# Two transformer layers, one new token each: what stays in SBUF between the layers

## Chip, cores and metric

One core of a Trainium2 chip runs the whole program. The metric is device time in microseconds of one execution; the kernel before has a median of 875.19 us in three runs.

## What is computed

Eight sequences (B=8) of one new token each, D=1024, go through the same two blocks twice, with the same weights and the same caches both times. All is float32.

```
for layer in 0, 1:
    n = layernorm(x)
    q = n @ wq                                   # 1024 x 4096, 32 heads of 128
    s = q . k_cache * 128**-0.5                   # 4 kv heads, 4096 positions; 8 query heads share one
    x = x + concat(softmax(s) . v_cache) @ wo     # 4096 x 1024
    n = layernorm(x)
    x = x + gelu(n @ w1 + b1) @ w2 + b2           # 1024 x 3584, 3584 x 1024
```

Each weight and each cache is read twice, once per layer. Per layer wq and wo are 16 MB each, w1 and w2 14 MB each, K and V 64 MB each (MB = 2^20 bytes), so 188 MB. SBUF holds about 24 MB at a time. Whatever is still there when layer 1 needs it isn't loaded again; the softmax has no mask, so the order in which batches are worked is free, and layer 1 goes through them backwards.

## The kernel before

**The arena.** One SBUF tile, `arena` (L110), is cut into units of 128 partitions x 1024 float32, 0.5 MB each. There are 52: 48 for loads (`N_TILE = 24` pairs) and 4 own ones, for score rows and probabilities. `Arena.take` (L62) hands out k adjacent units, those freed longest ago first; a `Slot` gives them back. A "piece" of a cache is two units: one kv head, half of the positions.

**The stream.** `stream` is a list of all loads in the order in which they are to be issued, built by `weights` (L495) and `caches` (L506). `pump` (L210) takes entries from its head while there is room, and issues a DMA for each on SP's queue (L221). It is called at each `release`, that is, where the program frees a tile. The program is written out beforehand, so the order on SP's queue is fixed; at run time each DMA waits until the engines that read its slot before have done so. One entry without room holds up all behind it.

**Compute.** Weight tiles stream through TensorE as the moving operand, with four groups of 32 output rows beside each other. `expand` (L237) multiplies the normed x with wq or w1, in two halves; `project` (L304) the heads with wo, or the hidden values with w2, tile by tile, and adds to x (L323). `scores` (L343) takes one piece of K in four matmuls (L352); after four pieces VectorE scales a half and takes the maximum (L357). `probs` and `turn` (L364, L376) make the softmax and turn the rows (L366 to L392), `values` (L393) takes a piece of V in four matmuls (L402), and VectorE puts the heads together (L405, L407, L414, L415). `layernorm` (L181) turns x and runs a mean; the variance is taken while the first matmuls of `expand` run. `plan` (L433) lists the steps of attention: for most batches all of K, softmax, all of V; for the last two or three of a layer K of one batch is mixed with V of the one before, with a lag of ten pieces.

**Loads.** In the attention of layer 0 a load is a whole batch's K or V, 8 MB, except for batches 6 and 7, which `CUTS` divides into 2 MB and 1 MB tiles. wo, w1, w2 of layer 0 and wq of layer 1 come in 1 MB tiles (a few of 0.5). In layer 1 the caches grow from 1 MB back to 8 MB, and wo, w1, w2 come in 16-, 14- and 8-unit tiles, with w2 ending in small ones.

**What is kept.** Between the layers 23 pieces stay: K and V of batch 7 and seven of the eight pieces of K of batch 6; one of them is parked in PSUM (`park_tile`, L478) and copied back later (`unpark`, L490). The last 1536 columns of wq stay in `spare` (L553). While they lie there, 4 units of the 48 and, once attention is over (`opened`, L486), the 4 own ones are left for the weights: a ring of 4 MB. Layer 1 starts with scores on kept pieces between the parts of its second half of wq (`early`).

x, b1 and b2 are loaded by three DMAs (x from ACT's queue, L129; the biases from SP's, L537).

Of the kernel before, what the change touches and what calls it, by code (L numbers as in the profile page):

```python
# [14 lines left out]
P = 128  # L15
# [6 lines left out]
CH = 512  # L22
# [11 lines left out]
LAG_V = 10  # L34

SCW = W // 2
N_TILE = 24
N_OWN = 2
EXTRA = 7
AT_ONCE = range(6), range(5)  # L40
CUTS = {
    (0, "k", 6): (2, 2, 2, 1, 1), (0, "v", 6): (2, 2, 2, 2), (0, "k", 7): (1, 1, 2, 1, 1, 2), (0, "v", 7): (2, 2, 2, 1, 1),
    (1, "k", 6): (2, 2, 2, 1, 1), (1, "v", 6): (1, 1, 2, 2, 2), (1, "k", 5): (1, 1, 1, 1, 2, 2), (1, "v", 5): (4, 4), (1, "k", 4): (4, 4),
}
# [6 lines left out]
class Arena:  # L51


    def __init__(self, ap):
        self.ap = ap
        self.low = 2 * N_TILE
        self.n = self.low + 2 * N_OWN
        self.freed = dict.fromkeys(range(self.n), 0)
        self.clock = 0
        self.limit = self.cap = self.low  # L60

    def take(self, k=1, own=False, pack=False):  # L62
        low = self.low if own else 0
        high = self.n if own else self.limit
        if k == 0:
            return Slot(self, 0, 0)
        able = [i for i in range(low, high - k + 1, k) if all(i + e in self.freed for e in range(k))]
        if not able:
            return None
        whole = lambda i: all(i // 4 * 4 + e in self.freed for e in range(4))  # L70
        i = min(able, key=lambda i: (pack and whole(i), max(self.freed[i + e] for e in range(k)), i))
        for e in range(k):
            self.freed.pop(i + e)
        return Slot(self, i, k)


class Slot:
    def __init__(self, arena, i, k):
        self.arena, self.i, self.k = arena, i, k
        self.cols = k * SCW  # L80
        self.ap = arena.ap[:, i * SCW:(i + k) * SCW]

# [6 lines left out]
class Kept:  # L89


    def __init__(self, ap):
        self.ap, self.cols = ap, ap.shape[1]
# [6 lines left out]
def decode_layers(ctx: ExitStack, tc: tile.TileContext, x, kc, vc, wq, wo, w1, b1, w2, b2, out):  # L100
# [9 lines left out]
    arena = Arena(const.tile([P, 2 * (N_TILE + N_OWN) * SCW], F32, name="arena"))  # L110
# [15 lines left out]
    x_row = const.tile([P, Q4], F32, name="x_row")  # L126
    bT = const.tile([P, NFT + NT], F32, name="bT")
    b1T, b2T = bT[:, 0:NFT], bT[:, NFT:]
    nc.scalar.dma_start(out=x_row, in_=x)  # L129
# [80 lines left out]
    def pump():  # L210
        while stream:
            key, k, src, limit, pack = stream[0]
            arena.limit = min(limit, arena.cap)
            slot = arena.take(k, pack=pack)
            if slot is None:
                return
            stream.pop(0)
            if callable(src):
                src(slot.ap)
            else:  # L220
                nc.sync.dma_start(out=slot.ap[:, 0:src.shape[1]], in_=src)  # L221
                slot.cols = src.shape[1]
            held[key] = slot

    def release(slot):
        slot.free()
        pump()
# [76 lines left out]
    def project(name, n_k, lhs, out_row, resid, rsum, hooks={}):  # L304
        y = ps_o.tile([P, CH], F32, tag="o", name="y")
        kt = 0
        for i, slot in enumerate(tiles(name)):
            for c in range(0, slot.cols, D):
                for j in range(4):
                    nc.tensor.matmul(y[32 * j:32 * j + 32, 0:Q4], lhs[:, kt * B:kt * B + 32],  # L310
                                     slot.ap[:, c + j * Q4:c + (j + 1) * Q4],
                                     start=(kt == 0), stop=(kt == n_k - 1))
                kt += 1
                if kt in hooks:
                    hooks[kt]()
                if name[0] == "p" and kt == 2 * NT:
                    add_b2(y)
                if kt == NR:
                    flush()
            release(slot)  # L320
            flush()
        assert kt == n_k
# [20 lines left out]
    def scores(at, kt, spare=False):  # L343
        b, j, half = at
        if j == 0:
            st["ps", half] = ps_o.tile([P, CH], F32, tag="o", name="s_ps") if spare else small_ps("s")
# [7 lines left out]
        if j == HKV - 1:  # L354
            if half == 0:
                st["row", b] = arena.take(own=True)
# [19 lines left out]
    def turn(b, half):  # L376
        row = st["row", b].ap
        if half == 0:
            st["S", b] = arena.take(own=True)
# [48 lines left out]
    def early(key):  # L428
        ap, done = ap_of(key)
        scores(key[1:], ap, spare=key[3] == 1)  # L430
        done()

    def plan(layer, order):  # L433

        steps = []
        for i, b in enumerate(order):
            n = i * NR
            whole = b in AT_ONCE[layer]
            steps.append((n + NR - whole, 1, ("probs", b)))
            steps.append((n + NR + 1 - 2 * whole, 2, ("turn", b)))  # L440
            for r in range(NR):
                steps.append((n + r, 0, ("k", *k_at(b, r))))
                steps.append((n + NR - 1, 3, ("v", *v_at(b, r))) if whole else (n + r + LAG_V, 3, ("v", *v_at(b, r))))
        steps.sort(key=lambda e: e[:2])
        return [key for _, _, key in steps]

    def attention(order, keep, done=(), hooks={}):
        ready = []
        steps = [key for key in plan(st["layer"], order) if key not in done]
        for n, key in enumerate(steps):  # L450
            if n == 0 and done:
                flush()
# [25 lines left out]
    def park_tile():  # L478
        spot = ps_k.tile([P, W], F32, name="spot")
        ap, done = ap_of(park)  # L480
        nc.scalar.activation(spot[:, 0:W // 2], ap[:, 0:W // 2], AF.Copy)
        nc.vector.tensor_copy(spot[:, W // 2:], ap[:, W // 2:])
        st["spot"] = spot
        done()

    def opened():  # L486
        arena.cap = arena.n
        pump()

    def unpark(ap):  # L490
        spot = st.pop("spot")
        nc.scalar.activation(ap[:, 0:W // 2], spot[:, 0:W // 2], AF.Copy)
        nc.vector.tensor_copy(ap[:, W // 2:], spot[:, W // 2:])

    def weights(name, dram, sizes, limit, short=(0, 0)):  # L495

        for u in range(dram.shape[0]):
            at = 0
            for i, k in enumerate(sizes[u]):
                n = min(k * SCW, dram.shape[2] - short[u] - at)  # L500
                key = ((name, u) if dram.shape[0] > 1 else name, i)
                stream.append((key, k, dram[u, :, at:at + n], limit[u], False))
                at += n
            assert at == dram.shape[2] - short[u]

    def caches(layer, order, skip):  # L506

        for key in plan(layer, order):
            if key[0] not in "kv" or key in skip:
                continue  # L510
            a, b = key[:2]
            lane = [(a, *(k_at if a == "k" else v_at)(b, r)) for r in range(NR)]
            at = lane.index(key)
            cuts = CUTS.get((layer, a, b), (NR,))
            starts = [sum(cuts[:i]) for i in range(len(cuts))]
            if at not in starts:
                continue
            m = cuts[starts.index(at)]
            name = (layer, key)
            for i, e in enumerate(lane[at:at + m]):  # L520
# [101 lines left out]
```

## Time and profile before

| what | us |
|---|---|
| median of 3 runs | 875.19 |
| lowest, highest | 874.1, 876.13 |
| span of the profiled execution (its own time is this span; no other time of it was taken) | 874.0 |
| TensorE busy in the span | 537.3 |
| VectorE busy | 182.3 |
| ScalarE busy | 48.8 |

The page gives, first, the busy time of each engine, then the span in 40 slices of 21.85 us with what the 16 DMA engines moved in each (GB/s). The chain of waits goes back from the last instruction to whatever released each step; in order of time its rows are: start in us, length in us, what it was (engine, tile, line, how many). In the timeline the bracket at a row's end says how long the engine had been idle and what ended that. In the table of windows the last three columns are the clock granted to TensorE (1.00 is full), the mean busy share of the DMA engines and GB/s. In a group of matmuls each matmul of the program appears twice, as float32 is worked in two passes.

### The profile page before, as it was taken

What the parts mean: (1) busy time and instruction counts of PE and PEld (TensorE: products, weight loads), DVE (VectorE), ACT (ScalarE), POOL (GpSimd) and SP (SyncE); (2) the same over time, 40 slices, a digit from 0 to 9 for tenths busy, and PEclk for the clock granted to TensorE, in tenths of its full rate; (3) what the DMA queues carried; (4) which work ended last, traced back from release to release, by engine and by line L of the source; (5) the groups of instructions that cost most, each with busy time, mean ns of one, the idle gap of its engine ahead of it and who ended that gap; (6) DMA issues with size and microseconds to landing.
All of it is one profiled execution on the core that took longest, in us unless ns stands there. A gap on an engine that the chain in (4) does not pass through costs nothing.

```text
span 874.0 us, 9060 instructions
## 1 busy us (share of the span) xinstructions
PE 537.3 (61%) x4000; PEld 179.4 (21%) x4000; DVE 182.3 (21%) x588; ACT 48.8 (6%) x76; POOL 1.7 (0%) x11
## 2 busy tenths in 40 slices
PE   0556665655657756666666879764665655665566
PEld 0212121211212212222221122211121211222223
DVE  0001232313122322200110134312232313120011
ACT  0110000000000100000000100000000000000000
POOL 0000000000000000000000000000000000000000
PEclk9977788777787977869978699886878777777878
DMA  9999999999999999999999999999999999999996
GB/s 389 434 432 430 432 439 439 438 436 436 432 430 406 426 426 426 403 407 419 421 421 412 418 423 432 431 445 430 439 432 433 430 432 430 433 432 436 426 424 287
DMA packets 19911, 370.22 MB, mean 424 GB/s; under 512 B 2464, under 2 KB 2720, under 8 KB 4128
## 3 DMA queue, kind: packets, MB, share of 16 engines
q1 hardware_dynamic: 19728, 369.52, 99.1%
q8 instruction: 31, 0.51, 0.2%
q10 hardware_dynamic: 144, 0.13, 0.0%
q14 instruction: 8, 0.07, 0.0%
HBM read 369.51 MB, written 0.13 MB: 423 GB/s over the span
## 4 chain that ended last, share of the span: by engine, by line
DMA 75%; PE 19%; DVE 4%; issue 1%; ACT 1%; SPq 0%; ACTq 0%; DVEq 0%
DMA arena<-in_A_v_cache_dram 25%; DMA arena<-in_A_k_cache_dram 24%; DMA arena<-in_B_w_dram 16%; PE sps L352 5%; PE o_ps L402 5%; DMA arena<-in_A_wo_dram 5%; PE acc L252 4%; DMA arena<-in_A_wq_dram 3%; DMA x_row<-in_A_x_dram 3%; PE y L310 2%; DVE scr L407 2%; PE sps L414 1%; PE sps L383 1%; DVE scr L405 1%; DVE arena L357 0%
## 5 line engine op out<-in xcount | busy, mean ns | idle before, releaser
L352 PE MATMUL sps<-arena,qz 128*32 128x512 f32 x992 | 146.1, 716 | 92.8 <-DMA arena<-in_A_k_cache_dram 82.7
L402 PE MATMUL o_ps<-arena 128*32 128x512 f32 x1024 | 155.5, 721 | 30.5 <-DMA arena<-in_A_v_cache_dram 30.4
L310 PE MATMUL y<-arena,oxT 128*32 128x256 f32 x960 | 80.4, 481 | 48.4 <-DMA arena<-in_A_wo_dram 29.6
L252 PE MATMUL acc<-arena,oxT 128*32 128x512 f32 (+3 forms) x522 | 77.8, 661 | 45.7 <-DMA arena<-in_B_w_dram 28.0
L407 DVE SCALAR_TENSOR_TENSOR scr<-o_ps,bits,scr 128x128 f32<-128x128 f32 x192 | 67.3, 350 | 6.8
L352 PEld LDWEIGHTS sps<-arena,qz 128*32 128x32 f32 x992 | 30.8, 125 | 181.6 <-issue 79.3
L310 PEld LDWEIGHTS y<-arena,oxT 128*32 128x32 f32 x960 | 34.2, 132 | 92.3 <-DMA arena<-in_A_wo_dram 32.3
L357 DVE TENSOR_SCALAR_CACHE_REDUCE arena<-sps 128x512 f32<-128x512 f32 x31 | 21.4, 691 | 151.4 <-PE sps L352 151.4
L402 PEld LDWEIGHTS o_ps<-arena 128*32 128x32 f32 x1024 | 31.2, 126 | 100.7 <-issue 65.4
L383 PE MATMUL sps<-ident,arena 128*128 128x128 f32 x128 | 29.9, 376 | 32.5 <-DVE oxT L415 16.8
L373 ACT ACTIVATE arena<-arena,bits 128x1024 f32<-128x1024 f32 x16 | 18.4, 1147 | 476.4 <-DVE scr L370 476.4
L414 PE MATMUL sps<-bits,scr 128*128 128x8 f32 x128 | 26.2, 277 | 28.5 <-DVE scr L407 24.8
L405 DVE TENSOR_SCALAR scr<-o_ps,bits 128x128 f32<-128x128 f32 x64 | 22.4, 351 | 91.6 <-PE o_ps L402 91.6
L252 PEld LDWEIGHTS acc<-arena,oxT 128*32 128x32 f32 x522 | 19.5, 122 | 95.2 <-issue 34.1
L414 PEld LDWEIGHTS sps<-bits,scr 128*128 128x128 f32 x128 | 20.4, 200 | 86.0 <-DVE scr L407 65.0
L383 PEld LDWEIGHTS sps<-ident,arena 128*128 128x128 f32 x128 | 19.3, 188 | 42.3 <-ACT arena L373 23.9
L415 DVE TENSOR_TENSOR oxT<-sps,scr 128x8 f32<-128x8 f32 x64 | 11.0, 171 | 79.8 <-PE sps L414 79.8
L389 DVE COPY arena<-sps 128x512 f32<-128x512 f32 x16 | 11.1, 691 | 44.1 <-PE sps L383 44.1
L184 PE MATMUL sps<-ident,x_row 128*128 128x128 f32 x16 | 4.0, 338 | 24.9 <-DMA x_row<-in_A_x_dram 23.2
L323 DVE SCALAR_TENSOR_TENSOR x_row<-y,x_row 128x256 f32<-128x256 f32 x4 | 1.7, 425 | 81.2 <-PE y L310 81.2
L391 PE MATMUL sps<-scr,bits 128*128 128x32 f32 x32 | 9.5, 388 | 12.5 <-DVE arena L389 12.5
L366 PE MATMUL sps<-scr,bits 128*128 128x128 f32 x32 | 7.8, 326 | 15.1 <-DVE scr L362 15.1
(71 smaller groups left out, 135.0 us busy)
## 6 DMA issues: line engine op xcount, KB each, us to landing
arena<-in_B_w_dram SPq DMA_DIRECT2D x27, 1024.0 KB, 8.4
arena<-in_A_v_cache_dram SPq DMA_DIRECT2D x10, 2048.0 KB, 29.2
arena<-in_A_wo_dram SPq DMA_DIRECT2D x15, 1024.0 KB, 8.6
arena<-in_A_k_cache_dram SPq DMA_DIRECT2D x7, 2048.0 KB, 29.5
arena<-in_A_wq_dram SPq DMA_DIRECT2D x14, 1024.0 KB, 8.0
arena<-in_B_w_dram SPq DMA_DIRECT2D x2, 7168.0 KB, 44.7
arena<-in_A_k_cache_dram SPq DMA_DIRECT2D x11, 1024.0 KB, 27.0
arena<-in_A_k_cache_dram SPq DMA_DIRECT2D x2, 4096.0 KB, 27.1
```

The source lines that it names most:

```text
L252: nc.tensor.matmul(acc[32 * j:32 * j + 32, d0 - starts[j]:d1 - starts[j]], xnT[:, kt * B:kt * B + 32], slot.ap[:, c + d0 - a:c + d1 - a], ...
L310: nc.tensor.matmul(y[32 * j:32 * j + 32, 0:Q4], lhs[:, kt * B:kt * B + 32], slot.ap[:, c + j * Q4:c + (j + 1) * Q4], start=(kt == 0), stop ...
L352: nc.tensor.matmul(ps[32 * g:32 * g + 32, :], qz[:, c:c + 32], kt[:, g * CH:(g + 1) * CH], start=(j == 0), stop=(j == HKV - 1))
L357: nc.vector.tensor_scalar(st["row", b].ap[:, half * CH:(half + 1) * CH], ps, SCALE, None, op0=ALU.mult, op1=ALU.max, accum_out=st["mx", b] ...
L373: nc.scalar.activation(row, row, AF.Exp, bias=bias, scale=1.0, accum_out=ls)
L383: nc.tensor.transpose(pp[:, t * P:(t + 1) * P], row[:, c:c + P], ident)
L389: nc.vector.tensor_copy(dst, src)
L402: nc.tensor.matmul(o[32 * g:32 * g + 32, :], s[:, g], v[:, g * CH:(g + 1) * CH], start=(half == 0), stop=(half == NH - 1))
L405: nc.vector.tensor_scalar(r, o[:, 0:P], sel_t[:, 0:1], None, op0=ALU.mult)
L407: nc.vector.scalar_tensor_tensor(r, o[:, t * P:(t + 1) * P], sel_t[:, t:t + 1], r, op0=ALU.mult, op1=ALU.add)
L414: nc.tensor.matmul(po[:, 0:REP], r_s[j % 2], sel_h, start=True, stop=True)
L415: nc.vector.tensor_tensor(oT_v[:, j * REP:(j + 1) * REP, b], po[:, 0:REP], rl_s[b % 2][:, j * REP:(j + 1) * REP], ALU.mult)
```

## The change

- The arena has 52 units with fixed places: `OWN = 48` to 51 for rows and probabilities, `RING = 32` to 47 (to 51 once attention of layer 0 is over). Each entry of the stream carries the list of units at which it may start.
- Kept between the layers: the first half of wq (units 0 to 15, loaded once at the start and read tile by tile in layer 1), K of batch 7 (units 16 to 31), and the first half of w2 (units 32 to 45, loaded last in layer 0). `Slot.keys` and `parts` turn a slot that is released into kept tiles instead of freeing it. One piece of the second half of wq is parked in PSUM and `spare` holds its last 1536 columns as before; `park` and `unpark` are now at wq's end.
- All cache loads are 4 MB (8 units, half of a batch's K or V), in four slots: 16, 24, 32, 40 in layer 0 and 0, 8, 16, 24 in layer 1. Only V of batch 7 in layer 0 ends in two 2 MB tiles.
- wo, w1 and w2 of layer 0 come in 2 MB tiles (with shorter last ones) through units 32 to 51; in layer 1 in 4 MB tiles through units 0 to 31.
- In layer 0 w2 is read second half first (`ks`), after both halves of the hidden values are there (`flush`); in layer 1 in order, so that the kept half comes first.
- Attention works whole batches only: K, softmax, V. `early`, `CUTS`, `AT_ONCE` and the lag are gone.
- x, b1 and b2 are put into one array beforehand and come in one DMA.

```diff
+N_UNIT = 52
+OWN = 48
+RING = 32
+R_AT = (46, 48, 50)
+KV_AT = (16, 24, 32, 40), (0, 8, 16, 24)
+HALF_AT = (32, 36, 40, 44), ()
...
+    def take(self, k, starts):
+        able = [i for i in starts if all(i + e in self.freed for e in range(k))]
...
+    def parts(self):
+        k = self.k // len(self.keys)
+        return [(key, Slot(self.arena, self.i + e * k, k)) for e, key in enumerate(self.keys)]
...
     def release(slot):
+        if slot.keys:
+            held.update(slot.parts())
+            return
         slot.free()
         pump()
...
+    def plan(order):
+
+        for b in order:
+            yield from (("k", *k_at(b, r)) for r in range(NR))
+            yield ("probs", b)
+            yield ("turn", b)
+            yield from (("v", *v_at(b, r)) for r in range(NR))
...
+    kept = {("k", *k_at(B - 1, r)) for r in range(NR)}
     orders = [list(range(B)), list(range(B))[::-1]]
+    ring = lambda k, i: range(RING, N_UNIT - k + 1, k)
+    deep = lambda k, i: range(0, RING - k + 1, 8 if k > 4 else k)
+    fixed = lambda *at: lambda k, i: (at[i],)
+    last_q = [2] * 5 + [2.5]
+    early = NFT // 2
+
+    weights(("q0", 0), wq[0], [16], fixed(0), kept=lambda i: [(("q1", 0), e) for e in range(8)])
+    weights(("q0", 1), wq[1], [16], fixed(RING))
+    stream.extend(caches(0, orders[0], (), {("v", B - 1): (4, 2, 2)}))
+    weights("o0", wo[0], [4] * 8, ring)
+    for u in range(2):
+        weights(("i0", u), w1[u], [4, 4, 4, 2], ring)
+    weights("p0", w2[0], [4, 4, 4, 2], ring, early * D)
+    weights("p0", w2[0], [4, 4, 2, 2, 1, 1], fixed(32, 36, 40, 42, 44, 45), 0, 4, lambda i: [("p1", i)])
+    weights(("q1", 1), wq[1], last_q, fixed(*R_AT, 0, 2, 4))
+    stream.extend(caches(1, orders[1], kept, {}))
+    weights("o1", wo[0], [8] * 4, deep)
+    for u in range(2):
+        weights(("i1", u), w1[u], [8, 6], deep)
+    weights("p1", w2[0], [4, 4, 2, 2, 1, 1], deep, early * D, 6)
...
+        ks = list(range(NFT))
+        if layer == 0:
+            flush()
+            ks = ks[early:] + ks[:early]
+        project(f"p{layer}", ks, hT, x_row, x_row, rsum)
```

More of the change, by code (lines that the diff above doesn't have):

```diff
@@ L506, in caches, with unpark @@
[L506 to L520, printed above, removed]
-                pieces[layer, e] = (name, i)
-            src = (kc if a == "k" else vc)[b]
-            yield (name, 2 * m, src[:, at * W:(at + m) * W], 2 * N_TILE, m == 1)
+    def unpark(key):
+        spot = st.pop("spot")
+        slot = arena.take(2, R_AT)
+        nc.scalar.activation(slot.ap[:, 0:W // 2], spot[:, 0:W // 2], AF.Copy)
+        nc.vector.tensor_copy(slot.ap[:, W // 2:], spot[:, W // 2:])
+        held[key] = slot
```

204 lines of the change are left out of this document (77 added, 127 removed).

## The prediction

> **What bounds the kernel now.** I read the first two parts of the page, then windows, then the chain of waits in order of time.
>
> ```profile
> span 874.0 us, 9060 instructions
> PE 537.3 (61%) x4000; PEld 179.4 (21%) x4000; DVE 182.3 (21%) x588; ACT 48.8 (6%) x76; POOL 1.7 (0%) x11
> ...
> GB/s 389 434 432 430 432 439 439 438 436 436 432 430 406 426 426 426 403 407 419 421 421 412 418 423 432 431 445 430 439 432 433 430 432 430 433 432 436 426 424 287
> DMA packets 19911, 370.22 MB, mean 424 GB/s; under 512 B 2464, under 2 KB 2720, under 8 KB 4128
> ```
>
> The 16 DMA engines move 370 MB at a nearly level rate, and no compute engine is busy for over 61%. In the windows below the DMA share is 1.00 and 1.01. So the kernel is one long transfer: the span changes only by what a byte costs, and by time in which the DMA queue is empty. The middle of the GB/s row (slices 12 to 23) is slower than its sides. That is the stage with short tiles. Two windows show it, and the last one the end:
>
> ```profile
> 40.00:240.00 200.00, 117.83 (x748) 37.49 (x752) 44.31 (x145) 11.96 (x17) 0.00 (x0) 0.76 1.00 432
> 390.00:460.00 70.00, 45.24 (x410) 16.36 (x414) 7.27 (x23) 3.93 (x7) 0.28 (x1) 0.87 1.01 420
> 860.00:870.00 10.00, 7.16 (x92) 3.63 (x92) 0.20 (x1) 0.00 (x0) 0.00 (x0) 0.83 0.71 292
> ```
>
> The last three columns are granted clock, DMA share and GB/s. At 390 to 460 us the DMA share is 1.01 although the ring holds only 4 MB: the small ring does not starve the engines there, the short tiles only carry less per unit of time. Prices per tile come from moments at which TensorE starts on a tile that has just landed, in the chain and, for 4 MB tiles, in the timeline of TensorE:
>
> ```profile
> 199.94 3.69 PE o_ps L402 x16
> ...
> 206.67 0.36 DVE scr L405
> ...
> 258.00 1.98 PE sps L352 x8
> ...
> 479.94 1.98 PE acc L252 x8
> ...
> 489.88 1.93 PE acc L252 x8
> ```
> ```profile
> 577.78 1.94 PE L352 MATMUL sps<-arena,qz 128*32 128x512 f32 x8 [6.03 <-DMA arena<-in_A_k_cache_dram]
> 587.49 1.06 PE L402 MATMUL o_ps<-arena 128*32 128x512 f32 x8 [2.42 <-DMA arena<-in_A_v_cache_dram]
> ```
>
> From 199.94 to 258.00 three 8 MB tiles landed: 19.35 us each. From 479.94 to 489.88 four 1 MB tiles: 2.485 each. A line through both is 2.409 us per MB (MiB) plus 0.076 us per tile; it gives 9.71 for 4 MB, and the two timeline rows are 9.71 apart. So a 2 MB tile is 4.89 and a 0.5 MB tile 1.28 (both worked out). The profile counts each matmul twice: "x32" is half a batch's K, 16 matmuls.
>
> **The change part by part.**
>
> *Bytes.* Layer 0 loads the same. Layer 1 loads, in columns of 512 bytes: before 31232 of wq, 215040 of caches, 90112 of wo, w1 and w2, together 336384; after 12800 of wq (half is kept, another part is in PSUM and the spare buffer), 245760 of caches (only one batch's K is kept), 75776 of the rest (half of w2 is kept), together 334336. That is 2048 columns or 1 MB less: -2.4 us. Much more weight is kept, and almost as much less cache.
>
> *Tiles.* The issues from SP's queue into the arena fall from 134 to 111, and the two for the biases go into the one for x: 25 fewer times 0.076 is -1.9. The cache tiles of 4 MB instead of 8 are in that count. Together -4.3.
>
> *The layers themselves.* In attention four 4 MB slots take the place of three 8 MB ones. A slot is refilled when TensorE has read it; three tiles of 9.71 us lie in between and the work on one takes under 15 us (5.64 and 8.46, below), so the queue stays full. The same holds for the 2 MB tiles of wo and w1, five slots of 4.89.
>
> *The handover from layer 0's last V to wo.* Here the queue can run dry. Half of wq sits in slots 0 to 15, the last batch's K in 16 to 31 and is kept, so the only room for wo is what the last V leaves in 32 to 47. Let t be the landing of the last half of K7. Behind it in the queue are V7 in 4, 2 and 2 MB: 9.71+4.89+4.89 = 19.5 us, and nothing else can be issued until the first V7 tile is read. That takes:
>
> ```profile
> 141.89 5.64 PE sps L352 x32
> 147.56 0.71 DVE arena L357 x2
> 148.31 3.69 PE sps L352 x32
> ...
> 638.53 0.71 DVE arena L357 x2
> ...
> 646.99 3.62 PE o_ps L402 x16
> ```
> ```profile
> out_dram<-x_row SPq DMA_DIRECT2D x1, 128.0 KB, 1.7
> ```
>
> Half of K after an idle time takes 5.64 us; the second half, without one, 3.69 (the granted clock averages 0.76 in the window 40 to 240). The softmax chain from L357 to the first value matmul is 8.46 (638.53 to 646.99). Four V pieces take 6.73 (199.94 to 206.67, where VectorE takes up the second head). Then SP issues, and the smallest transfer lands 1.7 us after its issue, of which I count 1.3 as time to the first bytes. So the first wo bytes move at t+5.64+8.46+6.73+1.3 = t+22.1, and the queue is empty from t+19.5: a stall of **2.6 us**. Ends: 0.7 with the half at 3.69, and nothing if the chain is 0.7 shorter too; with 1.4 us of delay above these rows, 4.0. In the kernel before finer tiles of two batches lie there. I take 2.6, since TensorE waits some 5 us for that half.
>
> The Trainium skill, TensorE: Matmul & The Clock Gate, section "HAM oscillation — how this bites in real kernels", says that a loop whose tile is computed faster than the next one arrives runs every tile at the low clock. It speaks against splitting K into halves that arrive apart; the rows above (5.64 against 3.69) agree, and by it the stall is 2.6, without it about 0.7. The skill's DMA: Bandwidth & Descriptors, section "Latency and other measured facts", puts the first byte at about 0.6 us for this path; by that page the stall would be 1.9, but the row of the output transfer says 1.7 to landing, and I keep it.
>
> *Stagger of the engines.* When the queue runs dry, engines that were ahead idle too and begin together again. In the window 860 to 870 the share is 0.71 before the last landing at 870.1: 2.9 us of mean stagger. What it costs has then been paid, and the engine that falls behind in the rest of the span pays again. Ends 0 and 2.9 times that rest's share (0.6) = 1.7; I take 0.5, nearer to nothing, since the span before already holds all delays of its slowest engine.
>
> *Between the layers.* Three places have cover, and cost nothing by these rows:
>
> ```profile
> 25.67 9.10 PE acc L252 x63
> ...
> 467.45 0.68 PE y L310 x8
> ...
> 470.12 1.05 PE acc L252 x4
> ```
>
> (a) Five loads of w2 and three of wq wait in SP's queue behind one slot, read out by the fourth w2 tile. If w1 ends at X, the four tiles land at X+4.9, 9.8, 14.7 and 17.2; the third and fourth are read by X+20.2 even at twice the 57 ns a record that the end shows (32 records 3.6, 16 records 1.8), bytes move by X+21.5, and the queue, with the fifth tile issued long before, lasts to X+22.1. (b) After w2's last landing three 1 MB tiles of wq run for 7.5 us. The first kept wq tile is read after 2.67 (467.45 to 470.12, the norm between) plus 1.1, and bytes move at 5.1. (c) V7's first load waits for the whole kept half of wq: 2.67+9.10+1.3 = 13.1; the queue lasts 7.5+5.0+3.1 = 15.6. Margins 0.6, 2.4 and 2.5 us. Behind (c) SP holds all further cache loads.
>
> *The end.* Only half of w2, 17.3 us of transfers, comes after w1, not 34. TensorE has to do its work in that time.
>
> ```profile
> 835.66 8.58 PE L252 MATMUL acc<-arena,oxT 128*32 128x512 f32 x64 [8.34 <-DMA arena<-in_B_w_dram]
> ...
> 853.47 0.75 PE L277 MATMUL sps<-ident,scr 128*128 128x128 f32 x4
> ...
> 855.38 3.66 PE L310 MATMUL y<-arena,oxT 128*32 128x256 f32 x64 [1.17 <-DMA arena<-in_B_w_dram]
> ...
> 860.50 0.39 PE L333 MATMUL y<-scr,bits 128*32 128x256 f32 x2
> ```
> ```profile
> 870.11 0.69 PE y L310 x8
> ```
>
> From w1's last landing v: the last 28 of 64 records 3.75, w2 by 224 records at 57 ns (3.66 over 64) 12.8, the turn 0.75, the bias 1.85 (from 859.04, where 855.38 ends, to 860.89): v+19.2. The transfers alone would allow v+17.3+0.7 (the 0.69 of the last tile) = v+18.0. So TensorE is late by **1.2**; ends 0 (with a quick start, as fast as the second half of those 64) and 4 (w2 as slow as the start of a tile after a wait).
>
> Sum: -4.3+2.6+0.5+1.2 = 0.0, so 874.0 for this execution's span of 874.0. What lies around the span is not changed. The execution stands 1.2 us under the median of 875.19; from the median the forecast is **875.2 us**.
>
> **The rivals.** (1) *The handovers are hidden.* TensorE is at speed when the last K half lands, wo starts 0.7 late, and the end is bound by transfers: -4.3+0.7 = -3.6, 871.6 us. For it: a 61% busy TensorE that has little left to do; against it the 5.64 row.
> (2) *Low clock at the handovers*, slower. The kept half of wq is read in eight pieces; rows 479.94 and 489.88 show 1.98 and 1.93 us a piece, where 25.67 has 9.10 for eight. At the slow rate V7's first bytes move at 2.67+15.6+1.3 = 19.6 instead of 13.1, 4.0 after the queue is empty. It decides once the eight take over 11.6 us (9.10 and the margin of 2.5). With 4.0 at the first handover and the rest as in the sum: -4.3+4.0+0.5+1.2+4.0 = +5.4, 880.6 us. Against it: unlike there, the pieces lie ready.
> (3) *The change doesn't do what it says*: the longer tiles are no cheaper, since the slow middle was that stage's and not the tiles'. Then the 1.9 us of the tiles is missing from the sum: +1.9, 877.1 us. The 9.71 row speaks against it.
>
> **How the numbers follow.** Forecast 0.50 (873.4 to 876.9), rival 1 0.22, rival 2 0.22, rival 3 0.06. A measurement of this kernel tells about 0.2%, 1.75 us, from no change. So faster 0.22, same 0.50, slower 0.28. The range leaves out the upper part of rival 2 and what lies under rival 1: 871.3 to 879.0. The forecast's own range is 873 to 877.
>
> **What would show it.** Right: the GB/s row level near 430 in the middle with one dip, where layer 0's attention ends; there TensorE waits for wo and SP's first wo issue follows the second V head by under 0.1 us; about 1 MB less moved; at the end TensorE runs without a wait into the last tile of w2. Wrong: no dip (rival 1), a second dip before layer 1's first V load (rival 2), about 420 GB/s in the attention windows (rival 3).

## The result, and the profile after

The kernel after takes 871.89 us (median of 5 runs, 871.26 to 872.87) beside 875.01 for the kernel before (5 runs, 874.10 to 876.13): a ratio of 0.9964, 95% interval 0.9951 to 0.9976. It is 3.1 us faster, where I had forecast no change. The spans of the two profiled executions differ by 3.4 us (874.0 and 870.6). The profiled execution of after took 872.42, 1.8 us more than its span; that distance is 1.7 to 1.9 in every later run too, so the execution of before, of which only the span is known, very likely took some 875.8. The prediction set its span of 874.0 beside the median of 875.19 and took the difference for an execution that was fast; most of it is this distance. As its sum was 0.0, the forecast doesn't change by that.

First the page of after: span, busy times, GB/s in 40 slices, DMA packets.

```profile
span 870.6 us, 9005 instructions
...
PE 554.2 (64%) x3988; PEld 191.5 (22%) x3988; DVE 182.6 (21%) x588; ACT 48.7 (6%) x76; POOL 1.7 (0%) x11
...
GB/s 391 434 434 433 432 434 428 425 434 431 427 431 431 433 434 425 388 429 430 424 409 411 436 431 431 434 433 432 429 431 428 432 431 428 431 433 430 429 425 291
DMA packets 16312, 369.17 MB, mean 424 GB/s; under 512 B 1809, under 2 KB 2065, under 8 KB 2577
```

As foretold, 1.05 MB (in millions; 1 MiB) less is moved, and the middle of the GB/s row is level but for dips (I had foretold one). The 388 in slice 16 (348 to 370 us) is the end of layer 0's attention; 409 and 411 (435 to 479) are the place between the layers. In between, where 1 MB tiles became 2 MB ones, the engines are as busy as before and carry more. Windows with granted clock, DMA share and GB/s at the end of each row, first of before, then of after:

```profile
370.00:450.00 80.00, 49.81 (x468) 17.30 (x472) 6.57 (x22) 3.93 (x7) 0.28 (x1) 0.86 1.01 416
```
```profile
370.00:450.00 80.00, 50.95 (x472) 20.39 (x468) 6.57 (x22) 3.93 (x7) 0.28 (x1) 0.82 1.01 428
```

More windows of after:

```profile
40.00:240.00 200.00, 130.96 (x774) 40.73 (x778) 47.19 (x151) 12.90 (x18) 0.00 (x0) 0.76 1.00 429
...
350.00:352.00 2.00, 2.00 (x13) 0.54 (x16) 0.36 (x1) 0.00 (x0) 0.00 (x0) 0.50 1.00 418
352.00:354.00 2.00, 2.00 (x12) 0.40 (x8) 0.35 (x1) 0.00 (x0) 0.00 (x0) 0.50 0.56 238
354.00:356.00 2.00, 1.73 (x16) 0.47 (x12) 1.23 (x5) 0.00 (x0) 0.00 (x0) 0.88 0.76 197
356.00:358.00 2.00, 1.46 (x16) 0.25 (x8) 1.23 (x4) 0.00 (x0) 0.00 (x0) 1.00 1.11 475
```

The dip is there, so the first handover isn't hidden outright. But it is small: shares of 0.56 and 0.76 over 2 us each and 1.11 behind them leave (0.44 + 0.24 - 0.11) x 2 = 1.1 us in which a DMA engine on average had nothing to do. What made it so small stands in the timeline of after (TensorE, VectorE and SP's queue; start, length, engine, line, what; in brackets the idle time before and what ended it):

```profile
336.68 5.34 PE L350 MATMUL sps<-arena,qz 128*32 128x512 f32 x32 [4.35 <-DMA arena<-in_k_dram]
...
342.07 0.69 DVE L355 TENSOR_SCALAR_CACHE_REDUCE arena<-sps 128x512 f32<-128x512 f32 x1 [8.97 <-PE sps L350]
...
349.94 5.01 PE L400 MATMUL o_ps<-arena 128*32 128x512 f32 x24
...
353.64 22.15 SPq L214 DMA_DIRECT2D arena<-in_wo_dram  x8
353.65 0.35 DVE L403 TENSOR_SCALAR scr<-o_ps,bits 128x128 f32<-128x128 f32 x1 [3.25 <-PE o_ps L400]
...
367.31 2.89 PE L308 MATMUL y<-arena,oxT 128*32 128x256 f32 x32 [2.63 <-DMA arena<-in_wo_dram]
...
396.73 1.93 PE L308 MATMUL y<-arena,oxT 128*32 128x256 f32 x32 [1.39 <-DMA arena<-in_wo_dram]
```

The last half of K7 lands at t = 336.68 and takes 5.34 us, as I had it. The chain from L355 to the first value matmul is 7.9 (342.07 to 349.94), not 8.46. The large miss is the next step. SP issues the first wo tile at 353.64, when VectorE takes up the *first* head of V7 (353.65), 3.7 us after the values begin. I had waited for the second head, 6.73 us. The program frees V7's 4 MB tile only when all four pieces are read. But the first wo tile is 2 MB and overwrites two of these pieces. In the built program the DMA waits only for the readers of what it overwrites. So the issue is at t+17.0, not t+20.8.

The rows also give what was lost there. Between 336.68 and the last wo landing, 396.73, are 60.05 us; V7 and eight wo tiles need 9.71 + 10 x 4.89 = 58.61. **The handover lost 1.4 us**, where I had 2.6 + 0.5. Below, "lost" is always this difference. The last part of the timeline is the end; the row below it is the DMA that SP issued at 834.25, w2's last tile, with the time from issue to landing:

```profile
849.48 2.78 PE L249 MATMUL acc<-arena,oxT 128*32 128x384 f32 x28 [0.26 <-DMA arena<-in_w_dram]
...
861.92 5.55 PE L308 MATMUL y<-arena,oxT 128*32 128x256 f32 x94
```
```profile
arena<-in_w_dram SPq DMA_DIRECT2D x1, 512.0 KB, 32.4
```

From w1's last landing (849.48) to the end of TensorE's work (861.92 + 5.55 = 867.47) are 18.0 us, not 19.2. The last 28 records of w1 took 2.78 instead of 3.75, and w2 made up the rest. My figure for transfers alone was 18.0 too, but that doesn't make the transfers the bound. TensorE goes through w2 without waiting for a load, as foretold, and the last tile lands at 866.65, just as TensorE comes to it: reading it takes about the last 0.8 us. In this execution both limits fall together.

So between the two profiles: -4.3 for bytes and tiles, +1.4 for the handover, nothing at the end; that is -2.9, beside the -3.4 of the spans and the -3.1 of the medians. Of the 2.9 between this and my 0.0, the handover is 1.7 and the end 1.2.

### The profile page after: what moved, and what is told of

It reads as the page before. It is cut to its first block, busy times and chain, and to the rows that moved or that the text cites. A ratio compares the mean times of both kernels' runs of the same rounds, so it can differ in the third digit from the quotient of the medians.

```text
span 870.6 us, 9005 instructions
## 1 busy us (share of the span) xinstructions
PE 554.2 (64%) x3988; PEld 191.5 (22%) x3988; DVE 182.6 (21%) x588; ACT 48.7 (6%) x76; POOL 1.7 (0%) x11
## 4 chain that ended last, share of the span: by engine, by line
DMA 75%; PE 20%; DVE 2%; issue 1%; ACT 1%; another core or an unknown queue 1%; SPq 0%; ACTq 0%; DVEq 0%
DMA arena<-in_k_dram 53%; PE sps L350 11%; DMA arena<-in_w_dram 10%; DMA arena<-in_wo_dram 7%; DMA arena<-in_wq_dram 6%; PE acc L249 3%; PE y L308 3%; PE o_ps L400 1%; PE sps L381 0%; PE sps L274 0%; DVE scr L405 0%; SPq L214 0%; ACT arena L371 0%; DVE arena L355 0%
## 5 line engine op out<-in xcount | busy, mean ns | idle before, releaser
L350 PE MATMUL sps<-arena,qz 128*32 128x512 f32 x1024 | 170.9, 827 | 103.4 <-DMA arena<-in_k_dram 102.1
L308 PE MATMUL y<-arena,oxT 128*32 128x256 f32 x960 | 75.9, 469 | 42.0 <-DMA arena<-in_wo_dram 30.9
L350 PEld LDWEIGHTS sps<-arena,qz 128*32 128x32 f32 x1024 | 42.2, 145 | 228.9 <-issue 182.4
L249 PE MATMUL acc<-arena,oxT 128*32 128x512 f32 (+3 forms) x510 | 71.1, 652 | 31.9 <-DMA arena<-in_w_dram 20.8
L355 DVE TENSOR_SCALAR_CACHE_REDUCE arena<-sps 128x512 f32<-128x512 f32 x32 | 22.1, 692 | 238.2 <-PE sps L350 238.2
L249 PEld LDWEIGHTS acc<-arena,oxT 128*32 128x32 f32 x510 | 21.5, 121 | 71.9 <-issue 34.1
L381 PEld LDWEIGHTS sps<-ident,arena 128*128 128x128 f32 x128 | 19.2, 187 | 43.4 <-ACT arena L371 27.7
L364 PE MATMUL sps<-scr,bits 128*128 128x128 f32 x32 | 7.8, 326 | 21.3 <-DVE scr L360 21.3
L181 PE MATMUL sps<-ident,xb 128*128 128x128 f32 x16 | 4.0, 338 | 25.1 <-DMA xb<-in_x_dram 23.4
```

Source lines behind the costliest of these rows:

```text
L249: nc.tensor.matmul(acc[32 * j:32 * j + 32, d0 - starts[j]:d1 - starts[j]], xnT[:, kt * B:kt * B + 32], slot.ap[:, c + d0 - a:c + d1 - a], ...
L350: nc.tensor.matmul(ps[32 * g:32 * g + 32, :], qz[:, c:c + 32], kt[:, g * CH:(g + 1) * CH], start=(j == 0), stop=(j == HKV - 1))
L355: nc.vector.tensor_scalar(st["row", b].ap[:, half * CH:(half + 1) * CH], ps, SCALE, None, op0=ALU.mult, op1=ALU.max, accum_out=st["mx", b] ...
L381: nc.tensor.transpose(pp[:, t * P:(t + 1) * P], row[:, c:c + P], ident)
```

## The experiments

Theory A: the gain is what bytes (2.4 us per MB) and tiles (0.076 us each) save, less what the handover still loses. In its first form it added that a moment in which only the DMA engines ahead of the others run dry costs nothing. Its rivals: the length of tiles is worth nothing, and the gain comes from other places; the handover is in the time as I had priced it; the handover is free.

Each kernel is the kernel after with the edit shown. The column "measured" is the ratio to the kernel before less that of after (0.9964 and, run again, 0.9975, mean 0.9970), times 875; it is uncertain by some 1.2 us. "Sum" is worked out from the number of tiles, the MB and the loss in the experiment's own trace, against a loss of 1.1 for after: in the four profiles whose layer 0 is the same up to there (after, again, p0slot, bytes1) it was 1.4, 1.0, 1.1 and 1.0. Each loss is that of one execution. The sum leaves out the end, where TensorE's work ended 0.8 us behind the last landing in after and 0.7 to 2.0 in the others.

| run | median us | ratio to before, 95% interval | measured us | sum us |
|---|---|---|---|---|
| again | 872.24 | 0.9975 (0.9964 to 0.9985) | | |
| split4 | 877.5 | 1.0032 (1.0021 to 1.0044) | +5.5 | +5.1 - 1.1 = +4.0 |
| bytes1 | 874.33 | 0.9997 (0.9988 to 1.0006) | +2.4 | +2.5 |
| wo8 | 875.02 | 1.0006 (0.9997 to 1.0015) | +3.2 | -0.1 + 4.8 - 1.1 = +3.6 |
| p0slot | 872.06 | 0.9968 (0.9957 to 0.9978) | -0.1 | 0 |
| k7first | 873.13 | 0.9990 (0.9979 to 1.0001) | +1.8 | +2.4 - 1.1 = +1.3 |
| whole8 | 869.93 | 0.9950 (0.9935 to 0.9965) | -1.7 | -2.1 + 0.9 - 1.1 = -2.3 |
| all3 | 871.90 | 0.9971 (0.9960 to 0.9982) | +0.1 | -2.0 + 2.8 - 1.1 = -0.3 |
| soft7 | 873.56 | 0.9989 (0.9980 to 0.9998) | +1.7 | +0.2 + 2.6 - 1.1 = +1.7 |
| best | 871.52 | 0.9966 (0.9953 to 0.9978) | -0.3 | -1.7 + 2.6 - 1.1 = -0.2 |
| k7half | 870.79 | 0.9957 (0.9944 to 0.9969) | -1.1 | +0.1 + 0.2 - 1.1 = -0.8 |
| whole8_p0 | 869.62 | 0.9940 (0.9927 to 0.9954) | -2.6 | -2.1 + 0.9 - 1.1 = -2.3 |

**split4: tiles of half the length.**

```
+            m = 4 * SCW if k == 8 else src.shape[1]
+            for c in range(0, src.shape[1], m):
+                nc.sync.dma_start(out=slot.ap[:, c:c + m], in_=src[:, c:c + m])
-            nc.sync.dma_start(out=slot.ap[:, 0:src.shape[1]], in_=src)
```

> The changed kernel with every 4 MB load issued as two 2 MB DMAs into the same slot; nothing else differs, and the slots stay as they are. 67 loads become 134. Theory A (a tile has a price of its own of 0.076 us even while the queue is full, so fewer tiles gave part of the gain): 67 x 0.076 = +5.1 us, about 877 against 871.9, landings of 2 MB 4.89 apart where 4 MB took 9.71. Theory B (the length of a tile is free while the queue is full, the gain came from bytes and from waits): no change, within 0.5 us.

Places, slots and bytes are the same, and it is 5.5 us slower: the number of tiles has a price by itself. In a window with a full queue and in the timeline:

```profile
40.00:240.00 200.00, 129.79 (x796) 39.71 (x800) 48.75 (x156) 12.90 (x18) 0.00 (x0) 0.80 1.00 425
```
```profile
338.88 3.25 PE L352 MATMUL sps<-arena,qz 128*32 128x512 f32 x16 [1.80 <-DMA arena<-in_k_dram]
...
354.30 6.36 SPq L216 DMA_DIRECT2D arena<-in_wo_dram  x3
...
397.57 1.93 PE L310 MATMUL y<-arena,oxT 128*32 128x256 f32 x32 [1.31 <-DMA arena<-in_wo_dram]
```

The DMA share is 1.00 as in after, at 425 GB/s instead of 429: the engines are as busy and carry less. Splitting had a gain as well: with only 2 MB of K left to read, SP issues wo 15.4 us behind the last K landing, and 397.57 - 338.88 = 58.69 loses nothing (V7 then needs 58.68). By that the time should be +4.0. Most of the other 1.5 is at the end of this trace:

```profile
853.18 4.48 PE L251 MATMUL acc<-arena,oxT 128*32 128x384 f32 x28 [2.17 <-DMA arena<-in_w_dram]
...
866.85 5.55 PE L310 MATMUL y<-arena,oxT 128*32 128x256 f32 x94
```

Here TensorE had waited 2.17 us for w1's last landing, the 28 records took 4.48 instead of 2.78, and its work ended 866.85 + 5.55 - 853.18 = 19.2 us behind that landing, 1.2 more than in after. That is the late TensorE of my prediction, in another kernel; the sum doesn't hold it.

**bytes1: 1 MB less is kept.** Two of the kept w2 tiles (1 MB) are loaded again in layer 1.

```
-    weights("p0", ..., 0, 4, lambda i: [("p1", i)])
+    weights("p0", ..., 0, 4, lambda i: [("p1", i)] if i < 4 else ())
...
+    weights("p1", w2[0], [2], deep, 12 * D, 4)
...
```

> The changed kernel keeping 6 MB instead of 7 MB of w2; the last 1 MB is loaded again in layer 1, so that it moves as many bytes as the kernel before. Theory A (each byte and tile has its price, and nothing hides it): +2.4 us for 1 MB and 0.1 for one more tile, +2.5, about 874.4. Theory B (the gain came from the handovers, a byte more or less is lost in the waits): under +1 us.

+2.4: the price of a MB holds.

**wo8: the first wo load overwrites the whole V7 tile.**

```
-    weights("o0", wo[0], [4] * 8, ring)
+    weights("o0", wo[0], [8] + [4] * 6, ring)
```

> The changed kernel with the first load of wo in layer 0 of 8 units instead of two of 4. It now overwrites all of the first V tile of batch 7, not its first half. Theory A (in the changed kernel the first wo load waits only for the two V pieces that it overwrites, 3.6 us after the values begin, and so the queue of the slowest DMA engine does not run dry): the first wo load is issued about 3.0 us later, the queue is empty for some 2 us, span +1.5 to +2.5 us. Theory B (as in the prediction: it waited for the whole V tile already): issue at the same place, no change beyond 0.3 us.

```profile
336.45 5.34 PE L350 MATMUL sps<-arena,qz 128*32 128x512 f32 x32 [4.29 <-DMA arena<-in_k_dram]
...
356.95 16.04 SPq L214 DMA_DIRECT2D arena<-in_wo_dram  x5
...
399.78 1.93 PE L308 MATMUL y<-arena,oxT 128*32 128x256 f32 x32 [1.65 <-DMA arena<-in_wo_dram]
```
```profile
354.00:356.00 2.00, 1.54 (x14) 0.46 (x10) 1.41 (x5) 0.00 (x0) 0.00 (x0) 0.91 0.10 41
```

This is my prediction's case made real: the wait is for all four pieces, the issue at t+20.5, the DMA share falls to 0.10. With after beside it, it shows that the wait goes by the part that is overwritten. And it shows that I had priced a late issue too low: 399.78 - 336.45 - 58.53 (one tile less) = 4.8 us are lost, where the rule of my prediction (issue + 1.3 - 19.5) gives 2.3. Theory A's own forecast, +1.5 to +2.5, was too low as well, since it let only the slowest engine count.

**p0slot: the dip behind w1 in layer 0.** The fourth w2 tile goes to a place that is free earlier.

```
-    weights("p0", w2[0], [4, 4, 4, 2], ring, early * D)
+    weights("p0", w2[0], [4, 4, 4, 2], fixed(32, 40, 48, 44), early * D)
```

> The changed kernel with the fourth w2 tile of layer 0 at unit 44 instead of 36, so that the loads behind it in SP's queue no longer wait until that tile has been read. Theory A (this wait lets the DMA engines run dry near 451 us and costs the 1.2 us by which the next w2 tile lands late): the dip there goes, -0.5 to -1.2 us. Theory B (only engines that are ahead run dry there, and the late landing is an instruction fetch): the dip goes, the time stays within 0.4 us.

Window 450 to 451 of after, then of p0slot:

```profile
450.00:451.00 1.00, 0.23 (x4) 0.00 (x0) 0.00 (x0) 0.00 (x0) 0.00 (x0) 0.97 0.76 311
```
```profile
450.00:451.00 1.00, 0.00 (x0) 0.00 (x0) 0.00 (x0) 0.00 (x0) 0.00 (x0) 1.00 0.93 393
```

The dip goes, the time doesn't move by anything that can be measured. The dip is some 0.2 us of mean engine time, so this doesn't tell whether it was free or only small. By the landings it may have cost more: the w2 tile behind it landed 6.1 us after the one before in after, 5.2 in again, 5.6 in bytes1 and 4.9 in p0slot, where 4.9 is the price of the tile.

**again, k7first, whole8, all3** ran on one chip.

> The kernel after once more, unchanged, as the base for the three others of this call. Both theories: 0.9964 of the kernel before, as it was measured first (0.9951 to 0.9976), so about 871.5 to 872.5 us.

**k7first** loads and scores K of batch 7 ahead of V of batch 6. The order of these two loads is changed with it, and K and V get two of the four slots each.

```
+        near = order[-2:] if st["layer"] == 0 else (None, None)
         for b in order:
+            if b != near[1]:
                 yield from (("k", *k_at(b, r)) for r in range(NR))
             yield ("probs", b)
             yield ("turn", b)
+            if b == near[0]:
+                yield from (("k", *k_at(near[1], r)) for r in range(NR))
             yield from (("v", *v_at(b, r)) for r in range(NR))
...
```

> Only the order at the end of layer 0's attention is changed: the last batch's K is loaded and scored ahead of the V of the batch before it, so that its softmax is over long before its V lands, and SP can issue the first wo tile before the queue of V tiles is empty. Bytes and number of tiles are the kernel after's. Theory A (engines that were ahead ran dry for a moment at the handover, and that cost nothing then, but the second wo tile came 1.4 us late): the dip at 352 to 356 us goes, DMA share 0.95 or more there, and the time falls by 0 to 1.4 us against the kernel after. Rival (the handover as I priced it, 2.6 us of stall and 0.5 of stagger, is in the time, and the gain of the change lies elsewhere): the time falls by 2.5 to 3.1 us.

```profile
336.60 1.07 PE L400 MATMUL o_ps<-arena 128*32 128x512 f32 x8 [3.13 <-DMA arena<-in_v_dram]
...
342.83 0.49 PE L364 MATMUL sps<-scr,bits 128*128 128x128 f32 x2
...
354.68 6.37 SPq L214 DMA_DIRECT2D arena<-in_wo_dram  x3
...
397.64 1.94 PE L308 MATMUL y<-arena,oxT 128*32 128x256 f32 x32 [1.47 <-DMA arena<-in_wo_dram]
```

Both forecasts were wrong: it is slower. The edit moved the loads and the scores, but left the softmax of batch 7 where it was, behind the V of batch 6 (L364 at 342.83). Now the last landing ahead of V7 is V6's second half, 336.60, and the first wo tile comes 18.1 us behind it: 397.64 - 336.60 - 58.61 = 2.4 us lost.

**whole8** loads the caches in 8 MB tiles in two slots.

```
+WHOLE_AT = (16, 32), (0, 16)
-                for m in cuts.get((a, b), (4, 4)):
+                for m in cuts.get((a, b), (8,)):
...
-    ... {("v", B - 1): (4, 2, 2)} ... {}
+    ... {("k", B - 1): (4, 4), ("v", B - 1): (4, 2, 2)} ... {("v", B - 1): (4, 4)}
```

> The caches are loaded in 8 MB tiles in two slots, where the kernel after has 4 MB tiles in four; only the last batches stay as they are. The same bytes in 28 DMAs fewer. Theory A (each DMA costs 0.076 us in a full queue, and two 8 MB slots are enough, since TensorE needs under 15 us for a tile that takes 19.35 to land): -2.1 us against the kernel after. Rival 1 (a tile's length costs nothing, the gain of the change came from the bytes and the places where the queue ran dry): 0.0. Rival 2 (two slots are too few: the next load is issued only when a whole tile is read, with 19.35 us queued ahead): dips in the DMA share in the attention windows and a time above the kernel after's.

-1.7 us; with **whole8_p0** (below), the same with p0slot's edit, -2.6. Theory A's -2.1 lies between them, the rival's 0.0 outside both. Two slots are deep enough: in whole8 the DMA share is 1.00 and the rate 432 GB/s from 40 to 300 us and again from 500 to 740.

**all3** is k7first, p0slot and 8 MB tiles together.

> Three edits at once on the kernel after: the last batch's K ahead of the V before it in layer 0, the fourth w2 tile in a place that is free earlier, and 8 MB cache tiles in two slots except for the last two batches of layer 0 (26 DMAs fewer). Theory A: -2.0 us for the tiles and 0 to -1.4 for the handover, so 0.9925 to 0.9945 of the kernel before, 868.5 to 870 us at a kernel before of 875. Rival (tile length free): within 0.5 us of the run with the order alone.

It gave nothing: the tiles' 2.0 us go to the later wo (issue 18.7 behind V6's second half, 2.8 lost).

**Where the loss begins.** Up to here the loss followed the delay d of the first wo issue behind the last landing ahead of V7, with a slope of one: d 15.4, lost 0.0 (split4); 16.9, 1.0 (again); 17.0, 1.4 (after); 18.1, 2.4 (k7first); 18.7, 2.8 (all3); 20.5, 4.8 (wo8). That is **d - 15.8**; whole8, p0slot and bytes1 lie on it too. Since the queue holds 19.5 us of transfers there, a DMA has to be issued 3.7 us before the last transfer ahead of it lands, or time is lost. I had said 1.3.

The traces also show what the 3.7 consists of. Three DMAs with the time from issue to landing, the first two wo tiles of after and the first of wo8:

```profile
arena<-in_wo_dram SPq DMA_DIRECT2D x1, 2048.0 KB, 7.3
arena<-in_wo_dram SPq DMA_DIRECT2D x1, 2048.0 KB, 10.6
arena<-in_wo_dram SPq DMA_DIRECT2D x1, 4096.0 KB, 11.9
```

In wo8, where the issue comes after the last V landing, the tile lands 2.2 us later than its 9.71 of transfer. So 2.2 is the way from issue to landing, apart from the transfer. In after the first wo tile was on time (353.64 + 7.3 = 360.9; K7's landing and the transfers give 361.1). The slowest engine did not stall. The second was 1.4 late (367.31 - 336.68 = 30.63 against 29.27). What the dip took was the lead of the other engines: V7's last tile landed on the first of the 16 engines at 352.76 and on the last at 356.03, the first wo tile between 360.51 and 360.93. At 365.2 one engine carried an instruction fetch of 16 KB for 1.0 us; of the second wo tile 15 engines were done at 365.82 and one at 367.26. The trace doesn't say that it is the same engine. But in k7half (below), which lost nearly nothing, the first wo tile still landed 3.2 us apart (357.65 to 360.85), and the same fetch at 364.4 delayed nothing. So some 1.5 of the 3.7 (an estimate, 3.7 - 2.2) is the stagger of the engines, which I had put at 0.5.

Four more runs tested the rule.

**soft7 and best**: K first again, but with the softmax of batch 7 between the V pieces of batch 6, and K7 and V7 in 2 MB tiles; best has the 8 MB tiles and p0slot's place as well.

```
+            if b == near[0]:
+                yield from (("k", *k_at(near[1], r)) for r in range(NR))
+                yield ("probs", near[1])
+            for r in range(NR):
+                yield ("v", *v_at(b, r))
+                if b == near[0] and r == 1:
+                    yield ("turn", near[1])
```

> The order of the run with K of the last batch first, mended: the softmax of the last batch is computed between the V pieces of the batch before it instead of behind them, and the last batch's K and V are loaded in 2 MB tiles, so that each waits only for 2 MB to be read (3 DMAs more than the kernel after, +0.23 us). SP should then issue the first wo tile by 349 us, seven us before the queue is empty. Theory A (the kernel after stands at the knee: its first wo tile arrives just in time, and some 0.9 us are given back there and later): -0.7 to +0.2 us against the kernel after, and no dip in the DMA share between 330 and 360 us. Rival (the 2.6 us that I priced are in the time of the kernel after): -2.4 us. Second rival (the run with K first lost its 1.3 us by the new order itself and not by the later issue of wo): +0.8 us or more again.

> That order together with 8 MB cache tiles in two slots for all batches but the last two of layer 0, and the fourth w2 tile in the place that is free earlier: 23 DMAs fewer than the kernel after. Theory A: -1.75 for the tiles and 0 to -0.9 for the handover, so 869.6 to 870.5 us beside 872.2 for the kernel after, the same as the run with 8 MB tiles alone (869.9) within the measurement. Rival (order costs by itself): 871 us or more.

```profile
327.05 3.63 PE L400 MATMUL o_ps<-arena 128*32 128x512 f32 x16 [5.51 <-DMA arena<-in_v_dram]
...
340.61 3.34 SPq L214 DMA_DIRECT2D arena<-in_v_dram  x2
...
349.66 12.41 SPq L214 DMA_DIRECT2D arena<-in_wo_dram  x4
...
398.02 2.94 PE L308 MATMUL y<-arena,oxT 128*32 128x256 f32 x32 [2.96 <-DMA arena<-in_wo_dram]
```

Both failed, and both by the rule. The rows are soft7's. SP issues wo in time now (349.66, with transfers until some 356), but the softmax between the pieces holds up V6's first half, and V7's second tile, which overwrites part of it, is issued only at 340.61. The transfers ahead of it end at 327.05 + 9.71 + 4.89 = 341.65, so it is 1.04 us ahead instead of 3.7: 2.7 should be lost. Lost are 398.02 - 327.05 - (9.71 + 12 x 4.89) = 2.6; in best it is 2.6 as well. The times are those of the rivals that blamed the new order, but by the trace the order costs through this late issue: the loss had moved to the DMA before.

**k7half and whole8_p0.** k7half takes up what split4 showed by the way: only the last 4 MB of K7 come in two tiles.

```
-HALF_AT = (32, 36, 40, 44), ()
+HALF_AT = {"k": (16, 20, 24, 28), "v": (32, 36, 40, 44)}, {}
-    ... {("v", B - 1): (4, 2, 2)}
+    ... {("k", B - 1): (4, 2, 2), ("v", B - 1): (4, 2, 2)}
```

> One DMA more than the kernel after: the last 4 MB of the last batch's K in layer 0 come as two tiles of 2 MB, so TensorE has only 2 MB of K left to read when the last of them lands, and the softmax begins sooner. Theory (in nine runs so far, the time from the last wo tile's landing back to the last K landing is longer than its transfers by the delay of SP's first wo issue behind that K landing, less 15.8 us): first wo issue at 15.3 to 15.6 us behind the last K landing instead of 16.9 to 17.2, nothing lost there instead of 1.0 to 1.4 us, and -0.9 to -1.3 us in the time (one more tile costs 0.08). Rival (only the slowest DMA engine counts, so that the handover was free already): +0.1 us. Rival (my prediction's rule from the Trainium skill, TensorE: Matmul & The Clock Gate, section on HAM oscillation: halves that arrive apart are read at the low clock, and the chain gains nothing): issue at 16.9 or later, +0.1 us.

> The run with 8 MB cache tiles in two slots, which had nothing lost at the handover (issue 15.3 us behind the last K landing), with the fourth w2 tile in the place that is free earlier besides. Theory: -2.2 us against the kernel after as the run with 8 MB tiles alone, and up to 0.4 us more for the dip behind w1 in layer 0: 0.9935 to 0.9955 of the kernel before. Rival (the low result of the run with 8 MB tiles was a matter of that call): 0.9965 or more.

```profile
336.46 1.92 PE L350 MATMUL sps<-arena,qz 128*32 128x512 f32 x16 [2.07 <-DMA arena<-in_k_dram]
...
350.11 9.91 SPq L214 DMA_DIRECT2D arena<-in_wo_dram  x5
...
395.26 1.93 PE L308 MATMUL y<-arena,oxT 128*32 128x256 f32 x32 [1.65 <-DMA arena<-in_wo_dram]
```

The issue comes 13.7 us behind the last K landing, earlier than I had said, and 0.2 us are lost instead of 1.1. The measured -1.1 fits; by itself it is no more than the uncertainty, and the verdict rests on the trace. It also answers the rule of the Trainium skill that the prediction weighed (TensorE: Matmul & The Clock Gate, section "HAM oscillation — how this bites in real kernels"). In k7half the last part, after a wait of 2.07 us, took 1.92 us at a granted clock of 1.00. In split4 the same 16 records, after a wait of 1.80, took 3.25 at 0.58. So the low clock came in one execution and not in the other. That section of the Trainium skill speaks of waits of over some 3.4 us, and these were shorter, so they don't contradict it. Beside the 5.34 of the whole half (clock 0.68) the split that I took the rule to speak against was worth 2.1 to 3.4 us on this chain.

whole8_p0 has the lowest time found, 869.62 us, 0.9940 of before (0.9927 to 0.9954); the intervals of whole8 and k7half overlap with it. Its profile beside that of whole8 shows how executions of the same instructions come to differ. whole8 first, then whole8_p0; up to here both are the same:

```profile
335.68 3.64 PE L351 MATMUL sps<-arena,qz 128*32 128x512 f32 x32 [3.24 <-DMA arena<-in_k_dram]
...
351.01 9.90 SPq L215 DMA_DIRECT2D arena<-in_wo_dram  x5
...
394.38 1.93 PE L309 MATMUL y<-arena,oxT 128*32 128x256 f32 x32 [1.64 <-DMA arena<-in_wo_dram]
```
```profile
335.64 5.34 PE L351 MATMUL sps<-arena,qz 128*32 128x512 f32 x32 [3.30 <-DMA arena<-in_k_dram]
...
353.12 6.36 SPq L215 DMA_DIRECT2D arena<-in_wo_dram  x3
...
396.01 1.93 PE L309 MATMUL y<-arena,oxT 128*32 128x256 f32 x32 [1.39 <-DMA arena<-in_wo_dram]
```

The same half of K took 3.64 us in one execution, at a granted clock of 1.00, and 5.34 in the other, at 0.68. The issue followed at 15.3 and 17.5, and 0.1 and 1.8 us were lost. The table takes their mean, 0.9, for both. whole8_p0 together with k7half's edit wasn't tried.

## Why the prediction was wrong, point by point

- **Bytes and tiles, -4.3: right.** bytes1 gave +2.4 for 1 MB, split4 +5.5 for 67 tiles more (5.1 by my price, with 1.1 less lost at the handover and 1.2 more at the end), the two runs with 8 MB tiles -1.7 and -2.6 for 28 fewer.
- **The handover, +2.6: the step that failed.** "Four V pieces take 6.73 ... Then SP issues" took the release of the whole slot for the wait of the DMA. The wait was for the two pieces that the 2 MB tile overwrites, 3.7 us. With 7.9 for 8.46 and 5.34 for 5.64 the issue came at t+17.0 instead of t+20.8. The stall of the slowest engine was not 2.6 but nothing: the first wo tile landed on time. wo8, where the DMA does overwrite four pieces, had the issue at t+20.5.
- **Stagger, +0.5, and 1.3 to the first bytes: both too small.** Together they held 1.8 us; the runs show that an issue has to lead by 3.7, some 2.2 for the way to the landing (wo8) and some 1.5 for the stagger. I had an upper end of 1.7 for the stagger and chose a value near nothing, since I took only the slowest engine for the bound. With t+17.0 and my own 1.3 the handover would have been free; it lost 1.0 to 1.4. That this is the lead of the faster engines, paid at the next instruction fetch, is read from the landings in after and k7half; no run changed the fetches, so it isn't tested. The Trainium skill's 0.6 us to the first byte (DMA: Bandwidth & Descriptors, section "Latency and other measured facts") would begin the loss at 18.9, further from the measured 15.8 than my 18.2. No run shows that part alone.
- **Between the layers, 0: right as far as the time tells.** Place (a), with the margin of 0.6, did dip (311 GB/s at 450 us); p0slot took the dip away, and the time stayed within the measurement, though the tile behind the dip landed 0.3 to 1.2 us late in three traces.
- **The end, +1.2: wrong in size for after.** TensorE took v+18.0, not v+19.2. The 28 records of w1 were priced at the rate of a tile that starts after a long wait; here the wait before them was 0.26 us and they took 2.78. The path itself stands: TensorE ran through w2 without waiting for a load, and in split4, where the wait was 2.17 us, it took v+19.2.
- **The rivals.** Rival 1, at 871.6 us, was nearest in time, but partly by luck. TensorE was not at speed when the last half of K7 landed (5.34 us at a clock of 0.68), the first wo issue was early for another reason, and 1.0 to 1.4 were lost instead of 0.7. At the end it let the transfers bind, where in after TensorE comes out at the same time. Rival 2 had its late issue only in wo8; its other place, the kept half of wq, took at most 8.1 us (469.35 to 477.42, clock 1.00) and not over 11.6. Rival 3 fell with split4.

My first form of theory A failed as well: it called the dip of the engines ahead free. Five of its forecasts (wo8, k7first, all3, soft7, best) missed for that reason or for an edit that moved the wait elsewhere.

## What to carry to other kernels

Where a kernel is one long transfer, price tiles and bytes from a full queue, then go to each place where the ring is shallow and ask three things: which bytes the next DMA overwrites, who reads *these* last, and how far ahead of the end of the queue that lets it be issued. Here 3.7 us ahead was needed, and each us less cost one. To win it, cut the last tile before a long serial chain in two, rather than reorder the chain: that costs one tile (0.08 us), while each reordering here delayed this DMA or the one before it.

## What the runs showed of the hardware that I had not expected

- To keep 16 DMA engines streaming at 430 GB/s the next issue had to lead the queue's end by 3.7 us, much more than the 1.7 us in which a small transfer lands.
- The 16 engines end one tile up to 3.3 us apart in a long stream (352.76 to 356.03 in after), and an instruction fetch of 16 KB holds one of them for 1.0 us. Where the spread was kept (k7half) the fetch delayed nothing; where a dip had closed it to 0.4 us (after), the next tile was 1.4 us late.
- The same 32 matmul records after the same wait of 3.3 us took 3.64 us in one execution (granted clock 1.00) and 5.34 in another (0.68).
- One thing that looks like the chip's doing is the program's: the semaphore wait of a DMA that overwrites half of a tile was over when that half had been read (353.64 in after), though the program frees the tile later; one that overwrites the whole waited 3.3 us longer (356.95 in wo8).
